# One DMA in place of nine TensorE transposes for the feature map of q, from the third batch on

## The chip, the cores and the metric

The kernel runs on one core of a Trainium2 chip. The metric is the device time of one execution in microseconds; before the change the median of three runs is 958.25 us (957.55 to 958.51).

## What is computed

Linear attention over 8 batches of 8 heads, 576 positions of width 64, feeds a dense mixture of 8 experts whose weights per token come from eight Sinkhorn rounds:

```
q_p, k_p = phi(q), phi(k)          # phi(x) = x + 1 where x > 0, else exp(x)
kv  = einsum('bhsd,bhse->bhde', k_p, v);   z = k_p.sum(axis=2)
attn = (q_p @ kv) / (q_p . z + 1e-6)        # -> x: 4608 tokens x 512
P = exp(x @ w_gate - max); 8 times: rows to sum 1, columns to sum N/E
out = sum over e of P[:, e] * (relu(x @ w1[e]) @ w2[e])
```

q, k and v are (8, 8, 576, 64) float32, w1 is (8, 512, 1024), w2 (8, 1024, 512), the output 4608 x 512 float32.

## The kernel before, in words

The kernel has a front, in which attention is computed and expert 0 is begun, and a long steady part, in which experts 0 to 7 run over nine groups of 512 tokens (`unit`, `block7`, `unit_plain`, lines 690 to 1120).

**The front.** `att(b, g)` handles a pair: four heads of one batch, two pairs per batch, 16 pairs in all. For a pair it loads k, q and v (L386; q and v are cast to float16 on the way), mostly from GpSimd's DMA queue. k goes through exp on ACT (L401) and two DVE operations (L405, L409), and 18 matmuls make kv (L430). Parts of it are cast into `kvz` on DVE or ACT (L339, L337). q goes through the same feature map (L474, L477, L480) into `tq`, laid out with positions on the partitions. The products with kv need it turned, with the head dimension on the partitions: TensorE transposes nine blocks of 128x128 into PSUM (`f_qt`, L485), and `f_qc` (L490, shown in the profile as the copy of L339 or L337) copies them into `qpT`. Then, in two column chunks each, TensorE makes the denominators ("den", PSUM tile `att`, L456), ACT takes ln and exp(-x) for the reciprocal (L508, L512), TensorE makes the numerators ("num", `num_ps`, L456), and DVE multiplies both into `xT` (L527). The first HB = 2 batches are cut into smaller pieces; from the third batch on q is handled in one piece and the columns are cut 288 + 288. `tq` and `qpT` have two buffers each, the inputs three each (`NV, NK, NQ`).

As tokens become complete, expert 0's first layer (L712, L736, PSUM `hq`) and second layer (L980, `ye`) are run between the attention's matmuls; its w1 and w2 are loaded in two halves each (L312). Every two batches the gate's logits are made (L544), and after the last of them the Sinkhorn rounds run. 40 dummy matmuls (L619) fill TensorE at the beginning.

**What sets the order.** `_Plan` collects every step as a task with an engine, a duration, dependencies and buffers. `_FRONT` is a list written out ahead of time (1n 118n ...: a task number and an engine letter); `run` emits the tasks in exactly that order, so the instruction order of each engine in the front is fixed, GpSimd's and SyncE's DMA queues included. An engine that waits holds up all that stands behind it. After the list is used up, the plan picks by its own costs and priorities. GpSimd's loads are planned with at most eight under way (`p_sw`).

SyncE's queue in the front holds the first loads of q and k, six little writes that wait for the last inputs (`f_gs`, L417), and then the stores of x and of its combinations into DRAM (`f_raw`, L759 and L760; `f_st`, L791), which expert 1 and later ones load back as `xs` (L809).

Of the kernel before, what the change touches and what calls it, by code (L numbers as in the profile page):

```python
# [11 lines left out]
FP16 = mybir.dt.float16  # L12
# [5 lines left out]
class _Plan:  # L18
# [121 lines left out]
    1n 118n 123n 621n 44s 45m 0g 42s 43m 2p 48g 49m 3p 4p 46g 47m 5p 80g 81m 6p 7p 78g 79m 8p 57n 58a 59d 9p 82g 83m  # L140
    60d 10p 84g 85m 11p 12p 50a 51d 13p 14p 15p 16p 17p 18p 52d 19p 20p 53n 54p 63a 64d 21p 55d 22p 93n 61p 65d 128g
    129m 56a 23p 94a 62d 24p 25p 130g 131m 66p 26p 67d 86a 132g 133m 87d 68p 27p 134g 135m 28p 95d 69a 29p 88d 30p
    119g 120m 99a 71p 96d 89n 100d 90p 72a 101d 70a 164g 165m 97p 91d 102p 98d 31p 92a 166g 167m 32p 73a 103d 74p
    143n 170g 171m 104p 136a 75d 33p 34p 137d 121g 122m 76p 35p 105a 36p 77d 37p 144a 38p 107p 138d 106a 110p 168g
    169m 39p 108a 40p 111d 41p 139n 149a 145d 140p 146d 147p 141a 200g 201m 622p 148d 142a 150d 109a 124g 125m 151d
    112p 623a 152p 113d 202g 203m 624p 172a 179n 173d 204g 205m 632p 153a 174d 180a 154p 228g 229m 181d 175n 176p
    155a 182d 625d 633a 183p 177d 630p 184d 178a 156a 190p 631d 160p 232g 233m 191a 634p 161d 192a 230g 231m 157p
    635d 185a 196p 626p 258g 259m 186d 158a 187d 636p 126g 127m 197d 627a 207d 188p 637a 654n 661p 189d 159a 193p
    162p 260g 261m 628p 163d 638p 213n 206a 194a 208d 262g 263m 195a 629d 198p 640p 662a 199d 214a 114g 115m 209n
    655p 215d 216d 210p 656a 286g 287m 235d 217p 211a 657p 218d 288g 289m 663p 241n 234a 212a 236d 658d 219p 316g  # L150
    317m 237n 238p 220a 243d 664d 242a 221p 290g 291m 239d 659p 222a 244d 667p 660a 265d 223a 245p 240d 669p 116g
    117m 246d 224p 247p 225d 639p 271n 264a 248a 318g 319m 668d 226p 646a 641p 266d 272a 344g 345m 273d 249p 267n
    642p 227d 320g 321m 670a 274d 250a 268p 346g 347m 648d 275p 269a 270a 644p 299n 276d 251a 252p 277p 645p 253d
    278a 293d 292a 643p 301d 279p 687n 254p 294d 372g 373m 280a 665p 255d 300a 295n 256p 666d 322a 302d 296p 323d
    329n 257a 652a 688p 324d 400g 401m 297a 303p 298a 650d 348g 349m 281a 282p 690p 304d 376g 377m 330a 331d 675p
    357n 374g 375m 283d 691a 305p 351d 402g 403m 284p 306a 676p 285d 325n 350a 307p 332d 326p 683d 308a 430g 431m
    359d 673p 327a 689a 328d 309a 352d 333p 310p 334d 674p 378a 311d 335p 671p 379d 336a 312p 358a 337p 313d 353n
    672p 338a 360d 432g 433m 354p 339a 404g 405m 385n 361p 407d 486g 487m 355a 692p 413n 362d 356a 434g 435m 681a
    694p 387d 386a 693d 363p 380d 342p 364a 696p 460g 461m 343d 695a 314p 388d 406a 415d 340p 677p 315a 341d 381n
    414a 389p 697d 436a 495s 488g 489m 382p 390d 458g 459m 416d 365p 383a 698p 437d 366a 462g 463m 443n 384a 678p  # L160
    408d 367a 579d 391p 370p 392a 700p 371d 699a 393p 685d 496s 368p 394a 702p 369d 409n 701a 706p 438d 720n 395a
    580d 410p 586d 703a 445d 679a 417p 521g 522m 587d 411a 581d 707p 471n 412a 418d 517g 518m 444a 398p 419p 399d
    721p 420a 519g 520m 446d 472a 396p 421p 397d 439n 704p 422a 465d 440p 423a 473d 474d 447p 490g 491m 441a 722d
    705p 529g 442a 448d 464a 424p 723p 425d 534n 449p 466d 426p 450a 725p 427d 467n 714a 451p 726d 468p 452a 497s
    524d 526s 453a 475p 712d 527s 710p 528s 502n 476d 469a 582s 583m 470a 711p 724d 503a 493d 456p 477p 504d 708p
    478a 457d 535a 727p 588d 505d 589s 590m 479p 584s 585m 729p 536d 480a 537d 454p 481a 709p 591s 592m 455d 428p
    728d 492a 484p 716a 731p 485d 429a 730a 538p 494d 732a 482p 718a 539d 733p 498n 523a 483d 506p 499p 507a 525d
    600d 530n 735p 500a 501a 601d 741p 734d 761n 602d 508p 736d 603s 604m 531p 509a 605s 606m 593d 510p 532a 594d
    762p 511a 533d 595d 742p 757d 512a 596s 597m 598s 599m 515p 540p 749a 516d 764p 541a 758d 513p 765a 542p 514d
    737p 543a 759d 743p 544a 763d 547p 607d 766p 548d 744p 767a 760d 545p 608d 751a 768p 546d 770p 577n 769a 800d  # L170
    738p 609d 771a 801d 610s 611m 753d 549p 612s 613m 802d 754d 772p 550a 745a 803s 804m 551n 552d 774p 805s 806m
    773a 739p 775a 578p 755d 776p 858d 740p 756d 777a 614g 615n 618n 619g 620m 778d 808p 807n 553p 810p 809a 779d
    782p 811a 780d 822p 554d 783a 781d 816p 747a 812p 555d 788p 813a 823a 814p 786p 815a 828p 817d 556p 818p 829a
    557d 784p 789a 859d 819d 832p 785a 558d 820p 824p 792p 825a 821a 790p 860d 830p 833d 861s 862m 616g 617m 559p
    826p 1031s 1032m 793d 866p 827a 1088s 1089m 834p 560d 863s 864m 787d 867a 794p 835a 831d 870p 795a 865n 836d 880p
    871a 840p 837d 881a 561d 882p 841a 872p 883a 886p 846p 887a 884p 847a 838d 868p 873a 890p 791d 869a 850p 891d
    885a 842p 916d 917d 876p 843a 918d 892p 877d 874p 893a 888p 851d 878p 875d 852p 879a 839d 924p 889d 844p 925a
    974d 930p 894d 845a 938p 975d 853a 562p 848p 976d 931a 895d 977s 978m 928p 979s 980m 849d 923n 898p 929a 563d
    896d 939a 900p 919s 920m 899a 897d 921s 922m 944p 564d 926p 904p 927a 942p 905a 932p 901a 934p 933d 940p 908p
    935d 941a 1023d 945a 565p 936p 909d 948p 937a 902p 949d 943a 566d 982p 903a 567d 946p 983a 910p 906p 950p 981n  # L180
    947d 986p 951a 988p 911a 952d 568p 996p 987a 998p 953d 956p 997a 569d 999a 907d 984p 957a 570d 1004p 985a 962p
    989a 1002p 958p 1003a 963a 1000p 954d 959a 992p 1005d 1006p 955d 966p 1007d 964p 967d 571p 993d 960p 1024d 994p
    1025d 990p 995a 968p 1026d 1001a 991d 1008p 1033n 1034p 965d 1009a 1022n 1544n 1036p 572d 1035a 1012p 573d 1037a
    1040p 1042p 1041a 1038p 1044p 1039a 1013p 969a 1045d 574p 1043d 1010p 961d 1046p 1027d 1048p 1047a 575d 1050p
    1049a 576d 1011p 1051a 1054p 856d 1056p 1019d 1055a 1052p 651d 686a 1058p 1028d 1016p 1018a 1029d 713a 1091p
    1059d 1053a 1014p 653d 1057d 1015p 647d 1017p 854d 1020a 1092a 1093p 1021d 1090n 1547n 1060p 1094a 1030d 1097p
    1145s 1146m 1061a 1099p 1095p 1062d 1066p 1063d 1068p 1064d 1067a 1098a 1065d 1071p 649a 1101p 717a 1069d 1076p
    1070d 1096a 1102d 715a 1079p 1078d 1072a 1077d 970a 1103p 1073g 748d 1105p 750d 1107p 1548g 1549m 1100d 1106a
    1082p 1108a 682d 1104a 1111p 1084d 1113p 1081d 1112a 1109p 1080d 1074a 1115p 1083d 1110a 1075g 1148p 1114d 746a
    1150p 1116d 1085p 1149a 1151a 1117p 1087d 1147n 1154p 1086d 1118a 1202s 1203m 1156p 857a 1119d 1152p 1123p 1155a  # L190
    1120d 972d 1125p 1124a 1121d 915a 1128p 1122d 680a 1127d 1158p 1129a 684d 1133p 1153a 1126d 1130g 1159d 1136p
    1545g 1546m 1135d 1134d 1160p 1138d 1162p 1157d 1164p 1163a 1139p 752d 1165a 796d 1161a 1168p 1141d 1170p 1140d
    1169a 1166p 1131a 1172p 1167a 1205p 1173d 1207p 1206a 1137d 1142p 1208a 1174p 1143d 1204n 1211p 1171d 1175a 1259s
    1260m 1213p 913a 1144d 1209p 1176d 1180p 1212a 1177d 1182p 1181a 1178d 719a 1185p 1179d 798a 1183d 1215p 1188a
    1184d 1190p 1210a 1216d 1186a 1214d 1193p 914a 1187g 971d 1217p 1191d 1132g 1219p 1192d 1221p 1189g 1220a 1196p
    1222a 1218a 1225p 1198d 1227p 1194d 1226a 1223p 1197d 1229p 797d 1224a 1262p 1228d 1264p 1263a 1230d 1199p 1265a
    1195d 1231p 1200d 1261n 1268p 1201d 1232a 1316s 1317m 1270p 973a 1233d 1266p 1237p 1269a 1234d 1239p 1235d 1238a
# [23 lines left out]
def kernel(  # L221
# [47 lines left out]
    NX = 5  # L269
    NS = 4  # L270
    NV, NK, NQ = 3, 3, 3
    HB = 2
    MG = 99
    xd = [dpool.tile([P, NXB], FP16, tag=f"xd{g}", name=f"xd{g}") for g in range(NG)]
    wg_sb = const.tile([P, NDT, E], FP16, tag="wg", name="wg_sb")
# [74 lines left out]
    def fadd(*a, **kw):  # L350
        t = add(*a, **kw)
        front_ids.append(t)
        return t
# [903 lines left out]
```

## Time and profile before

| | before |
|---|---|
| median of three runs | 958.25 us |
| the profiled execution | 958.06 us |
| its span | 955.9 us |
| TensorE busy (matmul) | 947.0 us, 99% |
| DVE busy | 784.1 us, 82% |
| ACT busy | 583.5 us, 61% |
| GpSimd busy | 146.8 us, 15% |
| TensorE's share of the chain that ended last | 95% |
| HBM read, written | 119.69 MB, 17.69 MB |

The profile is one execution as the hardware profiler saw it. Busy times are per engine; PE is TensorE, PEld its weight loads, which overlap the matmuls, and POOL is GpSimd. A group of instructions is written as line, engine, operation, output <- inputs, shapes and count, with the mean duration of one. In a timeline each row has the start and the busy time of a run of equal instructions, and in brackets the idle time before it and what ended it. The chain that ended last follows the work back from the end, at each step to what released it. DMA issues are listed with the size of one in KB as written and the median time from issue to landing.

### The profile page before, as it was taken

The numbers are of one execution on the slowest core, as the hardware profiler recorded it, in microseconds if no ns is written. First come the engines' busy times: TensorE is split into PE (matmuls) and PEld (weight loads), VectorE is DVE, ScalarE is ACT, GpSimd is POOL, SyncE is SP. The second block draws the span as 40 slices with busy tenths as digits, with TensorE's granted clock in tenths as the row PEclk, the third lists the DMA queues.
The fourth block names the chain that finished last, engine by engine and source line by source line (L and its number), as shares of the span: only waits on it lengthen the run. The fifth ranks groups of instructions, "written<-read, shape, count | busy, mean of one in ns | idle before, by whom it ended". The sixth has DMA issues, their size and how long they took to land.

```text
span 955.9 us, 21249 instructions
## 1 busy us (share of the span) xinstructions
PE 947.0 (99%) x8634; PEld 810.4 (85%) x8634; DVE 784.1 (82%) x1508; ACT 583.5 (61%) x1047; POOL 146.8 (15%) x211
## 2 busy tenths in 40 slices
PE   8999999999999999999999999999999999999998
PEld 4765588788888888888888888888888888888886
DVE  7899999998888888878887888878887888877775
ACT  7999766576555555555555555555555555555552
POOL 7432000011102111211112111110112111111110
PEclk9999999999999999999999999999999999999999
DMA  9998492172127222542227222362226222235554
GB/s 239 265 230 179 167 251 79 39 159 68 66 75 162 76 79 78 131 113 79 79 77 167 79 78 78 95 149 77 79 78 132 95 69 73 72 99 166 166 166 110
DMA packets 47101, 112.81 MB, mean 118 GB/s; under 512 B 4444, under 2 KB 27484, under 8 KB 47004
## 3 DMA queue, kind: packets, MB, share of 16 engines
q1 hardware_dynamic: 21340, 75.84, 24.1%
q0 software_dynamic: 25264, 35.11, 19.5%
q8 instruction: 67, 1.10, 0.5%
q10 hardware_dynamic: 400, 0.52, 0.2%
q14 instruction: 30, 0.25, 0.1%
HBM read 119.69 MB, written 17.69 MB: 144 GB/s over the span
## 4 chain that ended last, share of the span: by engine, by line
PE 95%; DVE 2%; DMA 1%; ACT 1%; POOL 0%; issue 0%; SPq 0%; DVEq 0%; ACTq 0%
PE ye L1098 36%; PE hq L858 24%; PE R L858 12%; PE Zye L858 6%; PE Zye L1098 6%; PE ye L980 4%; PE hq L736 2%; PE hq L712 1%; DMA w<-in_moe_w_dram 1%; PE kv_ps L430 1%; PE att L456 1%; PE num_ps L456 1%; PE att L485 1%; DMA kin<-in_k_dram 0%; DVE xT L527 0%
## 5 line engine op out<-in xcount | busy, mean ns | idle before, releaser
L1129 DVE SCALAR_TENSOR_TENSOR acc<-ye,P_sb,acc 128x256 f32<-128x256 f32 x620 | 267.7, 479 | 123.2 <-PE ye L1098 121.8
L858 PEld LDWEIGHTS <-W 128*128 128x128 f16 x2144 | 209.8, 98 | 24.9
L1098 PEld LDWEIGHTS <-S 128*128 128x128 f16 x1984 | 194.1, 98 | 22.5
L1139 POOL TENSOR_TENSOR acc<-acc,st 128x256 f32<-128x256 f32 x124 | 88.5, 733 | 686.5 <-ACT st L1136 686.5
L1098 PE MATMUL ye<-T,S 128*128 128x256 f16 x1488 | 192.8, 273 | 0.0
L858 PEld LDWEIGHTS <-w 128*128 128x128 f16 x1608 | 157.3, 98 | 19.6 <-issue 0.5
L1098 PEld LDWEIGHTS <-h 128*128 128x128 f16 x1584 | 155.0, 98 | 18.1 <-issue 0.2
L893 ACT ACTIVATE h<-hq 128x512 f16<-128x512 f32 x134 | 80.1, 598 | 141.9 <-PE hq L858 139.2
L858 PE MATMUL R<-xs,W 128*128 128x256 f16 x1008 | 151.2, 273 | 0.0
L858 PE MATMUL hq<-xs,W 128*128 128x256 f16 x1008 | 151.2, 273 | 0.0
L858 PE MATMUL hq<-xs,w 128*128 128x256 f16 x1008 | 140.9, 273 | 0.3 <-DVE h L896 0.3
L890 ACT ACTIVATE h<-Zye 128x512 f16<-128x512 f32 x134 | 80.1, 598 | 40.0 <-PE Zye L858 40.0
L1136 ACT ACTIVATE st<-Zye,P_sb 128x256 f32<-128x256 f32 x124 | 52.6, 471 | 71.1 <-PE Zye L1098 70.9
L873 ACT COPY Zye<-hq 128x512 f32<-128x512 f32 x134 | 77.7, 580 | 27.9 <-PE hq L858 27.7
L880 ACT COPY s<-hq 128x512 f32<-128x512 f32 x126 | 73.5, 583 | 34.6 <-PE hq L858 34.0
L1069 DVE TENSOR_TENSOR S<-h 128x1024 f16<-128x1024 f16 x124 | 85.4, 688 | 11.2 <-ACT h L893 11.1
L896 DVE CUSTOM_DVE_ANT_0 h<-R,s 128x512 f16<-128x512 f32 x126 | 86.6, 687 | 9.4 <-ACT s L880 9.4
L896 DVE CUSTOM_DVE_ANT_0 h<-hq,s 128x512 f16<-128x512 f32 x126 | 86.6, 687 | 3.5 <-PE hq L858 3.4
L858 PE MATMUL Zye<-xs,w 128*128 128x256 f16 x504 | 75.6, 273 | 0.0
L887 ACT COPY s<-R 128x512 f32<-128x512 f32 x126 | 74.5, 591 | 0.1
L1098 PE MATMUL ye<-w,h 128*128 128x256 f16 x528 | 68.4, 273 | 0.0
L1098 PE MATMUL Zye<-w,h 128*128 128x256 f16 x528 | 68.4, 273 | 0.0
(124 smaller groups left out, 988.7 us busy)
## 6 DMA issues: line engine op xcount, KB each, us to landing
xs<-xd SPq DMA_DIRECT2D x63, 896.0 KB, 4.8
kin<-in_k_dram POOLq DMA_DIRECT2D x15, 576.0 KB, 7.1
out_dram<-acc SPq DMA_DIRECT2D x67, 128.0 KB, 2.4
w<-in_moe_w_dram POOLq DMA_DIRECT2D x16, 512.0 KB, 8.8
w<-in_moe_w_dram POOLq DMA_DIRECT2D x7, 1024.0 KB, 13.0
vv<-in_v_dram POOLq DMA_DIRECT2D x16, 288.0 KB, 7.4
qin<-in_q_dram POOLq DMA_DIRECT2D x12, 288.0 KB, 7.8
xd<-acc SPq DMA_DIRECT2D x5, 512.0 KB, 3.4
```

Of the source, the lines that this page charges most:

```text
L858: nc.tensor.matmul(dst[:, p, :], lhsT=lhs(p, c), rhs=rhs(c), start=(first and p == 0 and c == 0), stop=(c == 1), skip_group_check=True)
L873: nc.scalar.copy(out=Zt[1], in_=gX["tile"])
L880: nc.scalar.copy(out=gs2["tile"], in_=gX["tile"])
L887: nc.scalar.copy(out=gs5["tile"], in_=gR["tile"])
L890: nc.scalar.activation(out=hd(0, 0), in_=Zt[1], func=AF.Relu)
L893: nc.scalar.activation(out=hd(1, 0), in_=gX["tile"], func=AF.Relu)
L896: nc.vector._custom_dve(TENSOR_ADD_SAT, out=dst, in0=ps, in1=sb, s0=3.0e38, s1=0.0)
L1069: nc.vector.tensor_tensor(out=Sx[:, i], in0=a0, in1=a1, op=op)
L1098: nc.tensor.matmul(bank(g_)[:, s, :], lhsT=lhs(s, kk), rhs=rhs(kk), start=(new and s == 0 and kk == 0), stop=(kk == 3), skip_group_check=True)
L1129: nc.vector.scalar_tensor_tensor(out=dst(), in0=bank(g_)[:, s, :], scalar=P_sb[:, gg, e:e + 1], in1=dst(), op0=ALU.mult, op1=ALU.add)
L1136: nc.scalar.mul(out=gst["tile"], in_=bank(g_)[:, s, :], mul=P_sb[:, gg, e:e + 1])
L1139: nc.gpsimd.tensor_tensor(out=dst(), in0=dst(), in1=gst["tile"], op=ALU.add)
```

## The change

For batches from TB = 2 on, `f_qt` and `f_qc` are not added. One `dma_start_transpose` on SyncE's queue takes all nine blocks of `tq` and writes them, turned, into `qpT`; its layout there is block by block, so den and num read it in runs of 64 columns with a step of 128, and the column cut becomes 256 + 320, whole blocks, for all batches. `HB` stays 2. The whole list `_FRONT` is replaced by another order, in which the tasks of GpSimd's queue also stand in another order: at the start k is loaded ahead of q on SyncE, and one load of k and two pieces of q more stand ahead of the first half of expert 0's w1. One dependency is added: `c1` also waits for the two matmuls that clear `Zt` (`t_zt`).

```diff
+    TB = 2
+    QDI, QDD, QDL = 1.0, 1.5, 3.0
...
-        cs = [(0, 256), (256, S - 256)] if b < HB else [(0, CH), (CH, CH)]
+        cs = [(0, 256), (256, S - 256)] if b < HB or b >= TB else [(0, CH), (CH, CH)]
...
-                nc.tensor.matmul(dst[:, hh, 0:cw], lhsT=gz["tile"][:, hh, z, :],
-                                 rhs=gq["tile"][:, hh, :, :].rearrange("p j w -> p (j w)")[:, c0:c0 + cw],
-                                 start=True, stop=True)
+                rhs = (gq["tile"].rearrange("p h j w -> p (h j w)").rearrange("p (j h w) -> p h j w", j=NJ, h=2)[:, hh, c0 // PW:(c0 + cw) // PW, :]
+                       if b >= TB else gq["tile"][:, hh, :, :].rearrange("p j w -> p (j w)")[:, c0:c0 + cw])
+                nc.tensor.matmul(dst[:, hh, 0:cw], lhsT=gz["tile"][:, hh, z, :], rhs=rhs, start=True, stop=True)
...
+            if b >= TB:
+                def f_qd(_):
+                    gq["tile"] = fp.tile([P, 2, NJ, PW], FP16, tag="qpT", name="qpT")
+                    nc.sync.dma_start_transpose(out=gq["tile"].rearrange("p h j w -> p (h j w)").rearrange("p (j w) -> p j w", j=NJ),
+                                                in_=gtq["tile"].rearrange("p j r d -> p (j r d)"))
+                t1 = fadd(("sp", QDI), f_qd, deps=[tm], acq=[gq], use=[gtq], prio=pr)
+                tq.append(fadd(("dma", QDD), lambda _: None, deps=[t1], use=[gtq, gq], prio=pr, lat=QDL))
+                continue
             t1 = fadd(("pe", 0.52 * sz), f_qt, deps=[tm, t_id[0]], acq=ga, use=[gtq], prio=pr)
...
-        c1 = add(("act", 0.58), f_seed, deps=[m1], acq=[gZ], use=[gX], prio=ui - 400.0)
+        c1 = add(("act", 0.58), f_seed, deps=[m1, t_zt], acq=[gZ], use=[gX], prio=ui - 400.0)
```

The new lines shift the line numbers behind them by up to six, and the shorter list shifts all by minus two or so: L712 becomes L718, L386 becomes L384, L485 becomes L483; L456 stays.

## The prediction

> **What bounds the kernel now.** I read the page's busy times first, then the busy time of each engine in stretches of 10 us, then the chain of waits over the first 34 us, then the engines' timelines there. The page's first part and the DMA row of its second:
>
> ```profile
> PE 947.0 (99%) x8634; PEld 810.4 (85%) x8634; DVE 784.1 (82%) x1508; ACT 583.5 (61%) x1047; POOL 146.8 (15%) x211
> ...
> DMA  9998492172127222542227222362226222235554
> ```
>
> TensorE is busy in 99% of the span, and the DMA engines are at nine tenths or more only in the first three slices, some 72 us, which is where this change works. The stretches of that stage (columns: start:end, length, then the engines' busy time, the granted clock, the DMA share and GB/s):
>
> ```profile
> 10.00:20.00 10.00, 8.54 (x82) 5.09 (x81) 8.55 (x18) 9.30 (x14) 6.09 (x9) 1.00 1.21 261
> 20.00:30.00 10.00, 9.36 (x98) 7.69 (x97) 8.14 (x17) 9.00 (x16) 6.55 (x9) 1.00 1.22 238
> 30.00:40.00 10.00, 10.00 (x109) 7.69 (x108) 8.59 (x14) 8.57 (x13) 4.19 (x6) 1.00 1.17 266
> 40.00:50.00 10.00, 10.00 (x97) 6.88 (x94) 8.72 (x15) 9.54 (x14) 4.20 (x6) 1.00 1.22 265
> 80.00:90.00 10.00, 10.00 (x93) 5.92 (x92) 9.67 (x18) 9.46 (x15) 3.07 (x5) 1.00 0.84 162
> 100.00:110.00 10.00, 10.00 (x92) 5.99 (x91) 9.35 (x19) 8.62 (x15) 0.00 (x0) 1.00 0.42 146
> ```
>
> From 30 us on TensorE has no gap. Whatever leaves its queue there comes off the end, and every wait put in there is added to it. DVE and ACT are near full, but TensorE does not wait for them. Before 20 us TensorE is filled with the 40 dummy matmuls of L619, so the kernel's own work starts when the first expert's weights arrive. The chain of waits shows it:
>
> ```profile
> 10.86 9.80 DMA w<-in_moe_w_dram
> 20.66 0.14 issue
> 20.80 1.03 PE hq L712 x8
> ```
>
> **Part 1: nine transposes and a copy go.** From the third batch on there are 12 pairs of heads, so 12 times nine matmuls of L485: in the instruction order of the changed kernel 108 of its 144 are gone. TensorE's timeline has what one set takes from its neighbours:
>
> ```profile
> 36.81 0.68 PE L485 MATMUL att<-ident,tq 128*128 128x128 f16 x9
> 37.32 1.91 PE L712 MATMUL hq<-xT,w 128*128 128x256 f16 x16
> ...
> 86.81 0.68 PE L485 MATMUL att<-ident,tq 128*128 128x128 f16 x9
> 87.32 1.03 PE L980 MATMUL ye<-w,h 128*128 128x512 f16 x4
> ```
>
> The next group starts 0.51 us after the first transpose (0.68 includes the pipeline's tail), so 12 x 0.51 = **6.1 us** leave a queue without gaps. The copies out of PSUM, 11 on DVE at 753 ns and one on ACT at 1120, go too; in the new order 11 casts of kvz move from ACT (365 ns) to DVE (422 ns). Neither engine is waited for by TensorE from 30 us on, so I count nothing for them. The cut of the 576 columns into 256 + 320 where it was 288 + 288 leaves the sum: TensorE paces 288 columns twice in 0.25 us and 256 and 320 in 0.22 and 0.27. A moving operand read in runs of 64 columns is already in L430, whose 18 matmuls of 192 columns take 0.92 us, 51 ns each; I count nothing.
>
> **Part 2: the new order starts later.** The order of the front is rewritten as a whole, POOL's DMA queue too. POOL's transfers land in the order of issue, and POOL waits for old ones to land before issuing more:
>
> ```profile
> 13.04 0.72 POOL L386 DMA_DIRECT2D qin<-in_q_dram  x1 [0.34 <-DMA vv<-in_v_dram]
> ...
> 17.86 0.71 POOL L386 DMA_DIRECT2D qin<-in_q_dram  x1 [0.95 <-DMA vv<-in_v_dram]
> ```
>
> The vv waited for at 13.04 is the sixth of POOL's transfers; counting KB written from the start, SyncE's two included, it ends at 2592 KB, and the first half of w1 (landed 20.66) at 4256 KB: 1664 KB in 7.62 us, 218 KB per us. In the new order one k of 576 KB and two pieces of q of 128 and 160 KB, 864 KB, and 4 KB of gate weights stand ahead of that half as well. That is 4.0 us at 218 KB per us, 3.3 at the 261 of the stretch 10 to 20; I take 3.6, so the first hq starts at 24.4 where it was 20.8. TensorE can't use the time: ahead of the first hq the new order has five transposes more, 0.28 us, and otherwise the same kv, den and num groups. Its waits for later halves need no more: by the same count the second half of w1 lands near 28.9 and is needed near 29.3, the halves of w2 near 35 and 46 for 36.7 and 47. Loss: 3.6 - 0.3 = **3.3 us**. Nothing behind it can win this back, as TensorE has no gap in which to catch up.
>
> **Part 3: the turn must land in time.** In place of 0.51 us plus a copy of 0.75 the den matmul (L456) waits for a DMA. Behind it on TensorE stands everything else, since each engine's order is fixed. What it has: qpT has two buffers, so a turn starts when the last num matmul of the pair two before is through, and must land by the den of its own pair. The new order gives TensorE's work in between, at 0.87 us for a group of hq or ye, 0.89 kv, 0.90 logits, 0.22 and 0.27 for a den or num of 256 and 320 columns. The tightest turn, the tenth, has hq, ye, den, kv, den, ye, hq, num: 4 x 0.87 + 0.89 + 0.22 + 0.27 + 0.22 = 5.1 us. All twelve, in order: 7.3, 6.7, 8.3, 6.8, 8.6, 6.9, 5.8, 6.9, 6.0, 5.1, 6.0, 5.2 us (the first two counted from where _FRONT puts the end of the feature map). If a turn takes t from free buffer to landing, TensorE loses the sum of t minus room over all turns that don't fit: 0 up to 5.1 us, 0.8 at 5.5, 2.0 at 6, 7.7 at 7, 11.5 at 7.4, 17.4 at 8, 64.5 at 12.
>
> No row shows a transposing DMA. The nearest rows:
>
> ```profile
> vv<-in_v_dram POOLq DMA_DIRECT2D x16, 288.0 KB, 7.4
> qin<-in_q_dram POOLq DMA_DIRECT2D x12, 288.0 KB, 7.8
> ...
> xd<-xT SPq DMA_DIRECT2D x9, 256.0 KB, 3.7
> ```
>
> The same queue moves 256 KB out of SBUF in 3.7 us, 288 KB then in about 3.8; the same bytes from POOL, in the saturated stage and behind other transfers of their own queue, take 7.4 to 7.8, the longest 12.0. I take 3.8 to 5, since nothing long stands ahead on SyncE's queue, and so **0 us**; the ends 3.8 and 12.0 stay for the range. The turns also write 12 x 288 = 3456 KB, 13 us of the DMA engines at 264 GB/s. Cover for the inputs: three buffers each at 5.95 us per pair (L485 from 36.81 to 102.25, 11 steps) against landings of 7 to 8 us. If it failed, each input would slip by up to 1.1 us. On SyncE the last two turns stand behind the gate's little writes (L417, at 92.5 to 93.3 us before, when the last transposes were still at 100.6 and 102.3) and the last behind a store of xd as well (two took 2.87 us to issue); its room of 5.2 us holds that 1.4 us with 3.8. The stores queued behind the turns serve the loads of xs, the first of which is issued at 133.6.
>
> Here the Trainium skill speaks against the change. VectorE: DVE Perf Modes, section The three transpose paths, gives 390 ns for a 128x128 transpose on TensorE and 1309 ns by DMA, and advises TensorE where PSUM will do. Its TensorE figure is not what this trace pays: 57 ns each in a run of nine. If its DMA figure held block after block, nine would be an estimated 11.8 us and the sum an estimated 1017 us, which is the far end of the third rival; DMA: Bandwidth & Descriptors, section Latency and other measured facts, gives 261 GB/s for such a DMA, an estimated 1.1 us for the bytes, by which the forecast holds. No row here decides between them.
>
> **Sum.** The profiled execution took 958.06 us (span 955.9 plus 2.16 around it), 0.19 under the median of 958.25, which I neglect. 958.06 - 6.1 + 3.3 + 0 = **955.3 us**.
>
> **Rivals.** (1) The start doesn't slip, because the first weights come as early as before: 958.06 - 6.1 = 952.0. For it: the queue is only reordered. Against it: 4256 KB ahead of a landing that TensorE waited for, and 5124 KB now. (2) The turn takes 5.5 to 6.5 us, as a landing beside a saturated stage may make it: 0.8 to 4.5 us of waits at den, 956.1 to 959.8, within the noise. (3) The other side: the turn is longer than its room. Place: den of L456 behind qpT; it decides from t = 6.5 us on. At 7.4, the median landing of the same bytes, 955.3 + 11.5 = 966.8; at 8, 972.7; at 12.0, the longest landing, 1019.8. For it: the stretches up to 80 us have a DMA share above 1, and t counts in every pair. Against it: SyncE's short landings. That the change doesn't do what it says is excluded by the instruction order.
>
> **Numbers.** Forecast 0.36; rival 1 0.08; rival 2 0.20; rival 3 0.36, of which 0.22 up to t = 8 and 0.14 beyond. A measurement of this kernel tells 0.2%, 1.9 us, from no change. Faster: forecast and rival 1, 0.44; within it: 0.20; slower: 0.36. The range goes from rival 1 to t = 8, 951.9 to 973; the forecast's own is 953.5 to 956.3.
>
> **What would show it.** Right: the first hq (now L718) waits for w until about 24; no waits of L456 for qpT from 35 us on; landings of the turns under 5 us; the end of the logits some 3 us earlier. Wrong: waits of att L456 for the DMA of qpT, one per pair, and SyncE busy with each turn for microseconds; or inputs that ACT waits for after 40 us.

## The result, and the profile after

The changed kernel takes 982.64 us (median of 4 runs, 980.88 to 983.98) against 958.16 of the kernel before on the same chip (4 runs): a ratio of 1.0255, 95% interval 1.0237 to 1.0274. It is 24.5 us slower. The prediction said 955.3, and at most 973.0.

The page of the changed kernel, its parts one to three:

```profile
PE 950.1 (97%) x8526; PEld 806.3 (82%) x8526; DVE 782.1 (80%) x1510; ACT 577.2 (59%) x1033; POOL 147.4 (15%) x211
...
PEclk9979899999999999999999999999999999999999
...
DMA packets 61308, 116.34 MB, mean 119 GB/s; under 512 B 18652, under 2 KB 41692, under 8 KB 61212
```

108 matmuls are gone, as the diff says, and yet TensorE's busy time has grown from 947.0 to 950.1 us. The reason stands in the row of the granted clock: its third and fifth slices (49 to 74 and 98 to 123 us) are not full. The other new thing is the packets: before there were 47101 of them, 4444 under 512 bytes; now 18652 are under 512, 14208 more. 12 turns x 128 partitions x 9 blocks are 13824 of them (the other 384 are of 4 bytes), so each turn is made of 1152 packets, and the trace lists them: 256 bytes each, on q1, the queue that SyncE issues to.

Stretches of 10 us of the stage (start:end, length, busy time and count of PE, PEld, DVE, ACT, POOL, then granted clock, DMA share, GB/s):

```profile
40.00:50.00 10.00, 4.28 (x75) 3.18 (x72) 5.08 (x9) 2.06 (x3) 2.42 (x4) 0.83 1.19 223
...
100.00:110.00 10.00, 5.08 (x27) 2.40 (x26) 5.36 (x10) 5.37 (x7) 1.68 (x2) 0.90 1.24 211
110.00:120.00 10.00, 10.00 (x68) 5.17 (x67) 6.44 (x12) 7.39 (x9) 0.70 (x1) 0.76 0.63 88
```

Where TensorE had no gap before, it now stands still for more than half of 40 to 50 and for half of 100 to 110. Behind the holes the clock is low: 110 to 120 is a stretch without a gap at 0.76 of the clock. The first hole in TensorE's timeline (start, busy time, what ran, and in brackets the idle time before it and what ended it):

```profile
51.42 0.58 PE L456 MATMUL att<-qpT,kvz 128*128 128x256 f16 x2 [6.91 <-DMA qpT<-tq]
51.94 1.62 PE L428 MATMUL kv_ps<-vv,t 64*128 64x192 f16 x18
...
55.71 1.55 PE L986 MATMUL ye<-w,h 128*128 128x512 f16 x4
59.26 0.38 PE L456 MATMUL att<-qpT,kvz 128*128 128x256 f16 x2 [2.00 <-DMA qpT<-tq]
```

The den matmul waits 6.91 us for its qpT. The groups behind it are slow as well: the same kv takes 0.92 us elsewhere and 1.62 here, the same ye 1.03 and 1.55. Then the next den waits again. Summed over the stage, TensorE's waits for these DMAs are (us in total, times, longest):

```profile
PE att L456 <- DMA qpT<-tq: 16.6, 5, 6.9
```

Seen from the turn's own line, L495 (counts, then duration of the issue in ns, min/median/max; then who waited for it; then the landing):

```profile
L495 SPq DMA_TRANSPOSE qpT<-tq x12: 1242/1942/7252, 37.2 to 128.5; - x12
...
  DVE tq L475: 3.2, 2
...
DMA to landing us min/median/max: 3.2/4.3/18.1
```

This last line rests on four of the twelve turns, as the trace names no landing for the other eight. Their packets are all there: the last packet of a turn ends 2.7 to 17.3 us after its issue. Seven of the turns need at most 5.3 us; five need more, those issued at 37.2, 41.0, 76.1, 90.3 and 95.5 us (13.2, 17.3, 8.1, 8.0 and 13.9 us), and these five are the ones that TensorE waits for: 6.9, 2.0, 0.3, 2.5 and 4.9 us. The first, issued at 37.18:

```profile
  PE att L456: 6.9, 1
```

The longest landing, 18.1 us, is that of the second turn, and the chain of waits between 36 and 59 us runs through it (start, length, what):

```profile
41.04 18.08 DMA qpT<-tq
```

**Where the 24.5 us of span came from.** I split each span at the first hq matmul and at the end of the last logits; in between, TensorE's time is at work or idle (the union of its matmul records). "Lost to half clock" is half of the time at work in which the clock record stands at 0.5, so it is worked out and not measured.

| us | before | after | whole rows instead (below) |
|---|---|---|---|
| up to the first hq | 20.8 | 25.4 | 24.1 |
| at work | 96.7 | 97.1, of which 6.8 lost to half clock | 90.5 |
| idle for qpT's DMA | 0 | 16.6 | 1.9 |
| idle for other things | 0.6 | 2.6 | 2.6 |
| behind the last logits | 837.8 | 838.7 | 838.6 |
| span | 955.9 | 980.4 | 957.7 |

### The profile page after: what moved, and what is told of

Its sections match the earlier page's. It is cut to its first block, busy times and chain, and to the rows that moved or that the text cites. A ratio compares the mean times of both kernels' runs of the same rounds, so it can differ in the third digit from the quotient of the medians.

```text
span 980.4 us, 21056 instructions
## 1 busy us (share of the span) xinstructions
PE 950.1 (97%) x8526; PEld 806.3 (82%) x8526; DVE 782.1 (80%) x1510; ACT 577.2 (59%) x1033; POOL 147.4 (15%) x211
## 2 busy tenths in 40 slices
DMA packets 61308, 116.34 MB, mean 119 GB/s; under 512 B 18652, under 2 KB 41692, under 8 KB 61212
## 3 DMA queue, kind: packets, MB, share of 16 engines
q0 software_dynamic: 25264, 35.11, 19.3%
## 4 chain that ended last, share of the span: by engine, by line
PE 88%; DMA 6%; DVE 3%; ACT 1%; issue 1%; POOL 0%; DVEq 0%; ACTq 0%; SPq 0%
PE ye L1104 35%; PE hq L864 24%; PE R L864 12%; PE Zye L864 6%; PE Zye L1104 6%; DMA qpT<-tq 4%; PE ye L986 3%; DMA kin<-in_k_dram 1%; DMA w<-in_moe_w_dram 1%; DVE xT L533 1%; PE kv_ps L428 1%; PE hq L742 1%; PE hq L718 1%; PE att L456 0%; PE num_ps L456 0%
## 5 line engine op out<-in xcount | busy, mean ns | idle before, releaser
L1075 DVE TENSOR_TENSOR S<-h 128x1024 f16<-128x1024 f16 x124 | 85.2, 687 | 11.8 <-ACT h L899 11.6
## 6 DMA issues: line engine op xcount, KB each, us to landing
w<-in_moe_w_dram POOLq DMA_DIRECT2D x7, 1024.0 KB, 13.2
```

What stands on the lines that cost most here:

```text
L1075: nc.vector.tensor_tensor(out=Sx[:, i], in0=a0, in1=a1, op=op)
```

## The experiments

Theory A, formed from this profile: a turn's 1152 packets of 256 bytes share every DMA engine packet for packet with the loads of POOL's queue (q0), so a turn beside the loads is slow by the number of its packets, and den's waits are the loss. Its rivals: any DMA on that queue beside the loads lands too late (B); the new order itself is worse (C); the transposing itself is slow, or gets in the way of other transfers (D); the DMA engines do only so many small packets (F). Some of the diffs are cut; "..." marks it. The ratios are to the kernel before, with 95% intervals.

### TensorE's transposes in the new order

```diff
...
-            if b >= TB:
-                def f_qd(_):
...
-                continue
```

In addition the list lets a task whose PSUM banks aren't free stand aside, and casts of kvz go back to ACT (the list changes accordingly).

> The changed kernel with its own order, but with the nine transposes on TensorE and the copy out of PSUM back in place of the DMA, at the same places of the order or at the first place behind it where the PSUM banks are free; the casts of kvz that had moved to DVE are back on ACT. Theory A (the loss is the turn's DMA, whose 1152 packets of 256 B alternate with the packets of the input loads): no waits of 2 us or more at den, the clock stays at 1.0, and what is left is the later start (first hq at 25.4 for 20.8): 963 us, 960 to 967. Rival C (the new order as such is the loss, whatever turns q): 975 or more.

Measured: 975.49 us (974.81 to 976.43), 1.0181 [1.0164, 1.0198]. Two of the longest sums of waits of TensorE in it:

```profile
PE att L461 <- DVE qpT L342: 2.8, 3, 0.9
...
PE num_ps L461 <- ACT kvz L340: 2.4, 3, 1.1
```

There is no wait of 2 us or more and no low clock, yet TensorE is idle for 12.0 us between the first hq and the last logits, in waits of up to 1.1 us, most of them for copies out of PSUM (qpT 5.2 us, kvz 2.5). The time is that of the rival and not of theory A. But the run doesn't tell what it was meant to: the order was laid out for a turn off TensorE, and the transposes, which need both banks of at2, stand in it wherever there was room. It shows only that the transposes in these places don't suit this order; whether they would in others is open. What the order itself costs under a DMA is seen from the next run.

### A plain copy in whole rows, and in 256-byte pieces

Whole rows, 128 packets of 2304 bytes a copy:

```diff
-                    nc.sync.dma_start_transpose(out=gq["tile"].rearrange("p h j w -> p (h j w)").rearrange("p (j w) -> p j w", j=NJ),
-                                                in_=gtq["tile"].rearrange("p j r d -> p (j r d)"))
+                    nc.sync.dma_start(out=gq["tile"].rearrange("p h j w -> p (h j w)"),
+                                      in_=gtq["tile"].rearrange("p j r d -> p (j r d)"))
```

> The changed kernel with a plain DMA from tq to qpT in place of the transposing one, same queue, same bytes, in rows of 2304 B; q is not turned, so that part of the computation is left out. Theory A (number and size of the packets): 128 packets a turn, landings of 3 to 5 us beside the loads, waits at den under 2 us in all, 955 to 960 us. Rival B (any DMA on that queue beside the loads lands too late): landings of 8 to 18 us and 975 us or more. Rival D (the crossbar is slow): as theory A here.

The same bytes in 1152 pieces, made so by a gap behind each block of qpT (den and num read it accordingly):

```diff
...
-                    gq["tile"] = fp.tile([P, 2, NJ, PW], FP16, tag="qpT", name="qpT")
-                    nc.sync.dma_start_transpose(out=gq["tile"].rearrange("p h j w -> p (h j w)").rearrange("p (j w) -> p j w", j=NJ),
-                                                in_=gtq["tile"].rearrange("p j r d -> p (j r d)"))
+                    gq["tile"] = fp.tile([P, NJ, 136], FP16, tag="qpT", name="qpT")
+                    nc.sync.dma_start(out=gq["tile"][:, :, 0:P], in_=gtq["tile"].rearrange("p j r d -> p j (r d)"))
```

> The same plain DMA, but cut into pieces of 256 B, 1152 a turn (qpT has its rows padded to 272 B so that they stay apart); q is not turned. Theory A: as slow as the transposing DMA, about 120 to 150 packets a microsecond beside the loads, landings up to 18 us, 972 to 985 us. Rival D (the crossbar is what is slow): as fast as with whole rows, 955 to 960 us.

Measured: rows 960.58 us (959.28 to 961.74, 10 runs), 1.0027 [1.0017, 1.0036]; pieces 973.16 us (972.36 to 977.06), 1.0166 [1.0145, 1.0186]. With rows the longest landing that the trace names is 6.6 us, above the 3 to 5 expected. TensorE's waits for the copy, with rows:

```profile
PE att L456 <- DMA qpT<-tq: 1.9, 1, 1.9
```

and with pieces, and their landing:

```profile
PE att L456 <- DMA qpT<-tq: 12.6, 5, 6.1
...
DMA to landing us min/median/max: 3.0/3.8/16.5
```

The two kernels have the same order, bytes and queue, and issue their first two copies within 0.3 us of one another; the number of packets differs, 128 against 1152, and with it the time by 12.6 us. The gaps in qpT differ too, but they don't slow what reads it: less the half clock, TensorE's work is 90.5 us with rows and 90.9 with pieces. Rival B falls with the rows, and so does C as the cause of the loss: the new order with a cheap DMA is within 2.4 us of before. Most of the loss needs no transposing at all.

But the order is not free. With rows, the table above has 6.2 us less work than before, and against it a start 3.3 us later, 2.0 us more of other waits, 0.8 more behind the last logits and 1.9 for the copy. By this account it would be at 955.8 without this last wait, in place of 955.9: a turn that never kept TensorE waiting would have brought next to nothing.

From the pieces to the transposing DMA there are 9.5 us more. In the spans of the two profiles (971.7 and 980.4) that is 4.2 of idle time, 3.4 of half clock and 1.6 of a later first hq, less 0.5 of work. The later first hq stands ahead of the first turn's issue, so it isn't the turn's doing, and its cause wasn't looked into. An issue of the transposing DMA holds SyncE for 1.24 to 7.25 us where one of the copy took 0.59 to 0.72. Which part of the rest the transposing as such has was not taken apart.

### The transposing DMA with short loads beside it

```diff
...
+                    jn = j1 if b < HB else 1
...
-                        out=dst.rearrange("p r j d -> p r (j d)")[:, :, D * j0:D * j1],
+                        out=dst.rearrange("p r j d -> p r (j d)")[:, :, D * j0:D * jn],
```

The source is cut likewise, and k and q of these batches reuse buffers already filled.

> The changed kernel with its transposing DMA, but from the third batch on the loads of k, q and v bring one ninth of their columns and the old contents of the buffers are computed with, so that the wide loads from GpSimd's queue are gone from the stage of the turns. Theory A: all turns land in 3 to 5 us, no waits at den beyond the first turn's, the clock stays at 1.0, 951 to 957 us (the later start stays). Rival D (the crossbar or the turn's issue on SyncE is slow by itself): waits at den of 10 us or more in all and 972 us or more.

Measured: 967.11 us (966.41 to 969.5), 1.0099 [1.0084, 1.0114]. The landings that the trace names, and TensorE's largest wait:

```profile
DMA to landing us min/median/max: 3.2/3.2/3.5
```

```profile
PE att L487 <- DVE tq L482: 5.1, 1, 5.1
```

The four landings that the trace names take 3.2 to 3.5 us, the last packets of all twelve end 2.7 to 4.0 us after the issue, no den waits for one, and SyncE's issue takes 1.24 to 1.42 us. So nine blocks in one transposing DMA are not slow by themselves: rival D falls as a cause of the long landings. The loads that are left on POOL's queue are nearly as many packets as before, 23920 against 25264 in the whole run, but 22.5 MB in place of 35.1. The time missed its forecast of 951 to 957, as it seems for a reason of the experiment: the feature map of an early q waits 5.1 us for its input (the reused buffers are the likely cause, not shown), and the first hq started at 30.2, 4.8 us later than in the changed kernel. From the first hq to the last logits it took 97.4 us, 18.9 less than the changed kernel's 116.3.

### Whose turn is it: two queues, smaller and larger pieces

Three more forms of the copy in pieces, den and num again reading it accordingly. Blocks 5 to 8 from ScalarE's queue:

```diff
...
-                    nc.sync.dma_start(out=gq["tile"][:, :, 0:P], in_=gtq["tile"].rearrange("p j r d -> p j (r d)"))
+                    src = gtq["tile"].rearrange("p j r d -> p j (r d)")
+                    nc.scalar.dma_start(out=gq["tile"][:, 5:NJ, 0:P], in_=src[:, 5:NJ, :])
+                    nc.sync.dma_start(out=gq["tile"][:, 0:5, 0:P], in_=src[:, 0:5, :])
```

> As the copy in 256-byte pieces (nothing is turned), but blocks 5 to 8 of each copy, 512 of its 1152 packets, are issued on ScalarE's queue instead of SyncE's. Theory A (the queues' packets take turns, one for one, on each DMA engine): the copy's two queues then get two packets for each one of the loads, so beside the loads the copy moves nearly twice the 140 to 150 packets per us that it had; the first two land after about 10 us instead of up to 16.5, the waits of den fall from 12.6 us to 3 to 6, and the time from 973.2 to 963 to 968. Rival F (the DMA engines do no more than some 145 small packets per us beside the loads, from whatever queue): still 140 to 150 per us, 971 to 975. A risk to both: ScalarE has to wait for the feature map before it can issue its half, which holds up its exp and ln.

Pieces of 128 bytes (a gap behind each half block):

```diff
...
-                    gq["tile"] = fp.tile([P, NJ, 136], FP16, tag="qpT", name="qpT")
-                    nc.sync.dma_start(out=gq["tile"][:, :, 0:P], in_=gtq["tile"].rearrange("p j r d -> p j (r d)"))
+                    gq["tile"] = fp.tile([P, NJ, 2, 68], FP16, tag="qpT", name="qpT")
+                    nc.sync.dma_start(out=gq["tile"][:, :, :, 0:D], in_=gtq["tile"])
```

> As the copy in 256-byte pieces (nothing is turned), with pieces of 128 bytes: 2304 packets a copy instead of 1152, the same bytes. Theory A (a packet of the copy waits for one of the loads' packets, whatever its size): still 140 to 150 packets per us beside the loads, so 16 us for each of the first copies, two queued 30 us and more; den waits 40 us and more, 995 to 1020. Rival F (the bytes or the total of small pieces' time count, so that half the size takes half the time): landings and waits as with 256 bytes, 971 to 977.

Two pieces per partition:

```diff
...
+                    src = gtq["tile"].rearrange("p j r d -> p (j r d)")
+                    nc.sync.dma_start(out=gq["tile"][:, 0:512], in_=src[:, 0:512])
+                    nc.sync.dma_start(out=gq["tile"][:, 520:1160], in_=src[:, 512:])
```

> As the copy in 256-byte pieces (nothing is turned), with two pieces per partition, 1024 and 1280 bytes, from two issues: 256 packets a copy. Theory A: 256 packets at 140 to 150 per us are 1.8 us beside the loads, between the rows of 2304 bytes (128 packets, 960.6) and the 256-byte pieces (973.2), much nearer the former: landings under 8 us, den waits 1.5 to 4 us, 960 to 963.5. If any copy in pieces is slow beside the loads, 966 or more.

Measured: two queues 968.94 us (968.85 to 971.3), 1.012 [1.0103, 1.0137]; 128 bytes 983.8 (981.3 to 985.21), 1.0265 [1.0249, 1.0281]; two pieces 961.29 (960.49 to 961.85), 1.0031 [1.0018, 1.0044].

The DMA queues of the changed kernel from 42 to 50 us (queue, packets, MB, share of the 16 DMA engines):

```profile
q0 software_dynamic: 1003, 1.52, 93.4%
q1 hardware_dynamic: 1005, 0.26, 24.9%
```

and of the copy on two queues from 41 to 45:

```profile
q0 software_dynamic: 489, 0.84, 83.6%
q1 hardware_dynamic: 489, 0.13, 21.4%
q10 hardware_dynamic: 463, 0.11, 12.8%
```

In these windows, in which each queue has something to send, each sends as many packets as the other: 1003 to 1005 here, 1322 to 1325 in the copy with 128-byte pieces from 41 to 49 us, whatever their sizes, and 489, 489 and 463 with a third queue. In the changed kernel the loads' packets carry 1518 bytes on average (1.52 MB in 1003), the turn's 256: with the same number of packets the turn gets a seventh of the bytes, 126 packets or 32 KB per us in that window, so its 288 KB take about 9 us.

Two things are not in this account. The counts stop being equal when fewer loads are left: from 51 to 58.4 us the loads sent 442 packets and the second turn 1087, which is still no more than 147 per us, and what held it there was not taken apart. And beside the loads the first packet comes 3.9 us after the issue of the first turn, 3.8 with the copy in rows, against 1.2 for the turn issued at 111.0 without loads; that part doesn't go by the number of packets.

Over two queues the copy moved 238 packets per us (952 in 4 us), against 136 on one queue in the same window of the copy in pieces (543 in 4 us): rival F falls. The Trainium skill states this in DMA: Bandwidth & Descriptors, section Queues, rings and completion order, in the words that each DMA engine "round-robins between the queue rows it has work for, at *packet* granularity". The rows above agree as to the turns, with one copied piece as the packet that is counted. The page puts about 9 to 17 descriptors in a packet; the trace doesn't tell how its pieces are grouped.

The number of packets then orders the times: 128 a copy 960.6 us, 256 961.3 (the runs of these two overlap), 1152 973.2, 2304 983.8. With 128-byte pieces I was too high (995 to 1020): the first copy's last packet ended 16.2 us after its issue, near the 16 foreseen, but by then POOL's loads had run out and the second went at 832 packets per us, not behind another 16 us of loads; it landed 15.5 us after its issue. The one on two queues stayed 0.9 us above its range, with 6.4 us of den's waits instead of 3 to 6.

### Only the last pairs by DMA, in the order of before

Pairs 14 and 15, then pairs 12 to 15; the other pairs keep the transposes and the order of before. The list again lets a task whose banks aren't free stand aside. Against the diff of the change, the number of the first batch differs:

```diff
-    TB = 2
+    TB = 7
```

> The kernel before with its own order, in which the last batch alone (pairs 14 and 15, whose transposes ran at 100.6 and 102.3 us, after the last input had landed) is turned by the transposing DMA. Theory A: with no input load in flight both turns land in 3.2 to 3.5 us, ahead of their dens, which stand 4 us behind: two sets of transposes less, 2 x 0.51 = 1.0 us, 957.1 us, ratio 0.9985 to 0.9995. Rival D (the crossbar is slow by itself): waits at den and 960 or more.

```diff
-    TB = 2
+    TB = 6
```

> The same for the last two batches, pairs 12 to 15; the transposes of pairs 12 and 13 ran at 86.8 and 92.0 us, while the last loads were still landing. Theory A: these two land in 5 to 9 us, where their dens stand 2 to 3 us behind, so 5 us or more of waits at den: 960 to 966 us. Rival (a turn costs the same wherever it stands): as fast as the one with two pairs or up to 1 us faster.

Measured: two pairs 957.31 us (956.84 to 957.8, 11 runs), 0.9991 [0.9982, 1.0000]; four pairs 959.39 (958.65 to 960.96, 11 runs), 1.0014 [1.0005, 1.0023]. With two, no den waits for a turn, and the 0.83 us between the medians are near the 2 x 0.51 that two sets of transposes take, though the interval reaches 1.0000. The profile doesn't put them there: of 0.8 us of span only 0.2 lie between the first hq and the last logits (0.8 less work, 0.6 more idle time), the others ahead of them and behind, where no transposes went. The third and fourth pair add up to a loss; in the profile with four pairs, which is of the slowest of its executions:

```profile
PE att L465 <- DMA qpT<-tq: 2.4, 2, 2.3
```

```profile
DMA to landing us min/median/max: 3.2/5.0/6.8
```

Pair 12's turn is issued at 85.5, with loads still on their way, moves 419 packets per us and is waited for; pairs 14 and 15, issued from 99 us on in the run with two, moved 741 and 753. The loss is smaller than the 960 to 966 I gave it.

### Two misses: w1 earlier, and matmuls to fill the waits

In the copy in whole rows, the first half of w1 was put ahead of five loads of POOL's queue, to win back the later start (the numbers are a task, g issues it and m is its landing; the list again lets tasks stand aside):

```diff
-    ... 63a 64d 166g 167m ... 35p 88d 119g 120m 98a ...
+    ... 63a 64d 119g 120m 166g 167m ... 35p 88d 98a ...
```

> The kernel with the plain copy in rows (960.6 us), and the first half of expert 0's w1 moved in GpSimd's queue to stand ahead of the loads of pair 3 and the v of pair 2; q is not turned. If the later start is what the new order loses by: first hq at 21 where it was 24.1, and 957 to 958 us. If the start costs nothing (the rest of the order gives it back): 960 to 961 us.

Measured: 962.79 us (962.26 to 963.3), 1.0047 [1.0033, 1.006], 2.2 us slower than the rows alone. The first hq starts at 27.6 instead of 24.1. TensorE's timeline:

```profile
24.57 0.58 PE L488 MATMUL att<-ident,tq 128*128 128x128 f16 x4 [1.64 <-DVE xT L538]
25.08 1.62 PE L433 MATMUL kv_ps<-vv,t 64*128 64x192 f16 x18
```

At 27.57 hq starts, and it no longer waits for w. What ended last is now the attention ahead of it: the load of q, pushed back in the queue, lands at 22.56, and eq, the reciprocal and xT follow from there. From 20.9 to 27.7 the clock is at half, and kv takes 1.62 us. So other loads of POOL's queue bind the start as well, not w1 alone.

In the changed kernel, 24, 6, 8 and 16 dummy matmuls ahead of the dens of pairs 4, 5, 10 and 11, to keep the clock up in the waits:

```diff
+                for _ in range({4: 24, 5: 6, 10: 8, 11: 16}.get(n, 0) if c == 0 else 0):
+                    nc.tensor.matmul(at2[:, 0], lhsT=warm[:, 0:P], rhs=warm, start=True, stop=True)
```

> The changed kernel with dummy matmuls (128x512, as L625) put into TensorE's order right ahead of the dens that waited longest: 24, 6, 8 and 16 ahead of the first den of pairs 4, 5, 10 and 11. They fill waits and compute nothing. If the half clock after the waits adds to the loss: the clock stays at 1.0, the work behind the second and the last wait runs at full speed, 4 us less, 976 to 980 us. If the clock costs nothing: 982 to 984 us.

Measured: 988.24 us (987.26 to 989.66), 1.0309 [1.0293, 1.0325], 5.6 us slower than the changed kernel. Its timeline:

```profile
44.52 5.34 PE L510 MATMUL att<-warm 128*128 128x512 f16 x24
51.53 0.38 PE L456 MATMUL att<-qpT,kvz 128*128 128x256 f16 x2 [1.66 <-DMA qpT<-tq]
51.84 0.92 PE L428 MATMUL kv_ps<-vv,t 64*128 64x192 f16 x18
...
57.91 0.38 PE L456 MATMUL att<-qpT,kvz 128*128 128x256 f16 x2 [1.74 <-DMA qpT<-tq]
...
73.18 0.58 PE L456 MATMUL att<-qpT,kvz 128*128 128x256 f16 x2 [4.89 <-DMA qpT<-tq]
```

Where the dummies stand they do what they should: the den comes at 51.53 as it did at 51.42, kv behind it takes 0.92 us instead of 1.62, and the ye that began at 61.99 begins at 59.76. Of these 2.2 us only 0.9 are the clock's: from the second turn's den to this ye it takes 1.85 us instead of 2.73. The other 1.35 come from that den, at 57.91 instead of 59.26, because its turn lands earlier, at 57.9 instead of 59.1. And what kv and the groups behind it gain at full clock is spent waiting for that same turn.

Being early then brings nothing: the next turn is issued at 61.8 instead of 63.7, beside loads that in the changed kernel were nearly over; it and the turn behind it move 267 packets per us together, where the changed kernel's next turn moved 802, and a new wait of 4.89 us with a new low clock stands at 73. The dummies also took 11.4 us of TensorE's time, and the waits for qpT fell only from 16.6 to 13.5. So the clock's share of the whole was not isolated by this run; that it costs time is shown in the one place, and 6.8 us in all is worked out from the clock record. Of these 6.8 us 2.7 lie between 51.4 and 56.8 us, ahead of the wait that ended at 59.26, and at full clock that wait would have been longer instead; so the clock itself added an estimated 4.1 us.

## Why the prediction was wrong, point by point

**Part 1, the transposes that go: right, but for a term put at nothing.** TensorE's work from the first hq to the last logits fell from 96.7 us to 97.1 - 6.8 = 90.3, or to 90.5 with the rows: 6.2 to 6.4, against the forecast 6.1 and the 0.3 of the five transposes that moved ahead of the first hq. The other cut of the columns and the reads in runs of 64 cost nothing that shows. DVE and ACT, counted at nothing, did not come out at nothing: TensorE's waits for them grew from 0.6 to 2.6 us, in the changed kernel as in the one with rows.

**Part 2, the later start: right in kind and nearly in size.** The first hq waits for w in the changed kernel too:

```profile
25.40 1.03 PE L718 MATMUL hq<-xT,w 128*128 128x256 f16 x8 [0.19 <-DMA w<-in_moe_w_dram]
```

It starts at 25.4 where 24.4 was forecast, at 24.1 and 23.8 in the two copies. That moving w1 forward in POOL's queue doesn't win the start back was not foreseen, nor that the part behind the last logits would take 0.8 to 1.1 us longer in all kernels with the new order; the latter was not looked into.

**Part 3, "The turn must land in time": the step that failed.** It said: "I take 3.8 to 5, since nothing long stands ahead on SyncE's queue, and so 0 us". Ahead of the first turn nothing did stand there, and yet its last packet ended 13.2 us after its issue; a turn alone is even quicker than forecast: 3.2 us. What was left out is that having a queue to oneself is not having the DMA engines: they served the two queues packet for packet, 1003 to 1005 in 8 us. The step took its landing from a transfer of SyncE's queue by bytes (256 KB, 3.7 us) without asking in how many packets those bytes went and what POOL's queue held at that moment; the stores behind this row are issued from 97 us on, behind the last input loads, and the turns from 37. It had the data: the stretches up to 50 us with a DMA share above 1. The second thing left out is that t is not one number: two turns are issued 3.9 us apart, the second sits behind the first, and its 18.1 us hold its own 8.0 of packets and the first one's 9.3. The two figures of the Trainium skill that were weighed there both fail as a price. By the one of VectorE: DVE Perf Modes, section The three transpose paths, nine blocks at 1309 ns would be an estimated 11.8 us, and alone they land in 3.2. By the one of DMA: Bandwidth & Descriptors, section Latency and other measured facts, the bytes take an estimated 1.1 us, which is in sight alone (1.5 us from the first packet to the last) and far off beside the loads.

**The third rival was right in its place, not in its price.** It put the loss at den of L456 behind qpT, with 0.36, and named the DMA share above 1, but not the packets. It reckoned that t counts in every pair; it counted in five of twelve, 16.6 us. That the measured time lies between its figures for t = 8 and t = 12 is luck: 10.7 of the 27.3 us above the forecast are no waits for turns. From 955.3 the way to the measured time is 16.6 for these waits, 6.8 for the half clock, 1.0 for the rest of the later start, 2.0 for other waits and 0.9 behind the logits: 982.6, against 982.64; the profiled execution itself took 983.32.

**Not in the prediction at all: the clock.** Before, the stage had it at 1.00 throughout. With three of the long waits the record stands at 0.5 for 10.2, 3.4 and 6.8 us (from 46.5, 60.2 and 108.0, the first and third while the wait lasts, the second just behind it); with the wait of 2.53 it doesn't. TensorE: Matmul & The Clock Gate, section What's actually happening, of the Trainium skill says that half speed follows an idle window of about 3.4 us, and full speed a busy one; the three lengths agree, being 3, 1 and 2 times 3.41 us, but the low clock begins only 2.0 us into the wait of 6.91, sooner than a whole idle window; there the record decides. The prediction priced a wait at its length; here the waits and the half clock come to 23.4 us together, of which 16.6 are the waits.

**"Cover for the inputs"** held: ACT waits for no input between 40 and 130 us. But the slow turn also holds `tq`, which has two buffers, and DVE waits 3.2 us in two places to write the next one.

## What to carry to other kernels

Price a DMA that runs beside a saturated queue by its packets, not its bytes: here it got one packet for each one of the neighbour's while the neighbour had loads to send, so 256-byte packets beside ones of 1.5 KB got a seventh of the bytes, and what lands in 3.2 us alone took up to 18 behind another of its kind. Take the row for the price from the stage in which the DMA will run. An operation taken off the bounding engine and put on DMA pays at most where the DMA engines have room; here that is the last two pairs, and the gain there is at the edge of the noise. Count what a new order costs by itself: here it took back all that the transposes gave. And a wait that is put on TensorE may cost more than its own length, as the matmuls behind it may run at half clock.

## What the runs showed of the hardware that was not expected

- Queues that all had work got equal numbers of packets: 1003 to 1005 on two, 489, 489 and 463 on three.
- A transposing DMA of 128 x 1152 float16 from SBUF to SBUF goes as 1152 packets of 256 bytes. With the short loads beside it its four named landings took 3.2 to 3.5 us, with SyncE's issue at 1.24 to 1.42; beside the full loads an issue took up to 7.25 us.
- The granted clock fell to half 2.0 us into a wait of 6.91, and rose again 5.3 us after its end.
